# A kernel of 2068 ordered operations: 52 of them at other places, one copy of work given to another engine

## The chip, the cores and the metric

One core of a Trainium2 chip runs the whole kernel. Its engines are TensorE (PE, matmuls; its weight loads are listed as PEld), VectorE (DVE), ScalarE (ACT), GpSimd (POOL) and SyncE (SP), which issues the DMAs. The metric is the device time of one execution in microseconds; the time of before is the median of three runs.

## The reference

x has 2048 rows of 512. It is normalised row by row; the normalised rows go through a linear attention with 32 heads of 16 and through a feed-forward block of width 1792, and the output is x plus the product of the two.

```python
xn = _layernorm(x, axis=-1)
# attention: qkv = xn @ wqkv, per head:
pq = jnp.einsum("bhsd,hdf->bhsf", q, w_phi)
phi_q = jnp.concatenate([_softmax(pq, axis=-1), _softmax(-pq, axis=-1)], axis=-1)   # phi_k from k likewise
kv = jnp.einsum("bhsf,bhsd->bhfd", phi_k, v)
z  = jnp.einsum("bhsf->bhf", phi_k)
o  = einsum(phi_q, kv) / (einsum(phi_q, z) + 1e-6);  s = o @ wo
# feed-forward: h = xn @ w1 + b1, act = h * tanh(softplus(h))  (Mish), then act @ w2
g = _silu(_B_ref(xn, w1, b1, w2))
return x + s * g
```

Everything is float32.

## The kernel before, in words

**Tiles.** The 2048 rows are 16 tiles of 128 rows, x0 to x15. For each tile the program loads x, forms mean and variance (mv), 1/sqrt (rs, a power on GpSimd), normalises x in place, transposes it on TensorE in four pieces into a PSUM bank (pt), and copies that to SBUF as a high part (ScalarE) and a remainder (VectorE), together xT. The high and low parts of both factors make one float32 product out of three matmuls of a 128x512 result; a product over half the depth is six matmuls.

**Fewer products.** k and v, and likewise the two matmuls of the feed-forward block, are formed from sums of tiles and sums of weights, so that seven products do the work of eight. The sums of tiles t and t+4 are ts, split into th and tl; those of the weights are ws, split into wss by ScalarE (high) and GpSimd (low), and w1s, split into w1sh and w1sl. The running sums in PSUM are kx, ky and kz for k and v, fx, fy and fz for the first matmul of the feed-forward block, x, y and z for the second. A bank is copied out between two products (for fx: ha, hb, hc and hd, in that order), and the product that follows adds to it, so it waits for the copy.

**Attention.** For each tile of v there is a tile with one more column block of ones, which gives the sum z. That block is written by a copy of its own, of 16 columns, before the copy of v itself:

```python
def v_tile(t):
    v = alloc("s2", [P, H + 1, DH], f"v{t}")
    vp[t] = v
    copy(v[:, H], ones[:, 0:DH])
```

q of each tile goes out to DRAM (qs, qd) and comes back in another layout (qp). Later ez and tz form the denominators, ph the transposed features, pn the numerators, oh and ol their split, pw the product with wo, and so its copy, which goes out to DRAM.

**Start and end.** The first instructions on TensorE are matmuls of a tile of ones (wake), whose result nobody reads. The weights of q and k are multiplied by the feature map first (the folds wkf and wqf, from phit). At the end each output tile takes silu of its sum, times s, plus x.

**Order.** The program is not issued as it is written. Each call of an engine is recorded as one operation (or some calls as one: a product of six matmuls, four transposes), 2068 in all, numbered as recorded. A list, SCHED, then gives the order of issue. Where an operation was recorded for two engines (a copy for ScalarE or VectorE, a subtraction for VectorE or GpSimd, a normalisation for VectorE or ScalarE), a letter behind the number says which takes it: V, A or G. Each engine runs its own operations in the order of the list; an engine waits at an operation until what it reads is written and what it overwrites is read. A second list, PLACE, gives each of the 945 tiles its buffer within its pool (slot, s2, st, sm, rq, tq, and ps for the eight PSUM banks):

```python
for s in SCHED.split():
    i = int(s.rstrip("VGA"))
    op = self.ops[i]
    e = s.lstrip("0123456789") or next(iter(op))
    for m, a, k in op[e]:
...
        getattr(g, m)(*a, **k)
```

All operations are issued from one line, 192 of the kernel before, so the profile tells them apart by the names of their tiles and not by lines.

Of the kernel before, what the change touches and what calls it, by code (L numbers as in the profile page):

```python
# [49 lines left out]
0 1 2 3 4 5 6 7 8 25 26 27 11 12 9 10 15 13 64 36 28 29 30 31V 67A 65 16 37 39A 44 14 17 94 72 18 45 46 47 32 68 69 33  # L50
40 41 38 48 49 66 50A 34 73 74 43A 19 75 96 51 95 42 148 99 22 76 128 192 283 20 71A 118 172 55A 77 149 78V 79 21 70
193 100 52 80 23 97 129 56 130 53 57V 83 84 121 214 194 131 150 268V 85V 173 81 469 470 196 101 132 197 174 59 98 215
216 133 134V 24 58G 152 122 378 242 161G 189G 119 243 195 244 217 102 198 123G 162 104 164 135 136 139A 86 471V 87 379
381 89 137 176 140 177 246 88 245 284 285 247 142G 178 141V 103A 218 105 153 199 175 165 238 239 240A 287 114 286 143
# [21 lines left out]
604G 697 814 843 844 709 710 711 749 1100 665 692 785 784 786 799 798 742 698A 722 723G 699 763 741A 686 590 684 889
815 756 1054 1053 853 801 800 757A 855A 743 941 750 943 942 944 945 700 733 734 736 685 851V 852 817A 854A 735 752 744
766 767A 759 751 819 818 881 701 901 883 728 997 880 885 820V 845 823 753 754 821 737 888 822 891 788 1137G 865G 760A
846A 764A 769 758 848 946 947 1138 1139 738 1140 739 755 849 1141 1102 1142 866 775 768 1143 867 770A 824A 776A 761
1144 765 772 777 1145 827 887 847 996 1104 825 874 877 875A 830 1103 868 869 773 886 1105 828A 870 904 878 906 910 920  # L80
1106 903 1107 948G 856G 905 1108 831 771 790 882 826 774 893 890 1196 829 988 921A 857 858 907 908 909 949 871 986 911A
957 896 922 987A 1011 1012A 832 876 884 973 850 789 1197 778 879 950 951 1160 872 1109 787 1043 923 912 894 1025G 859
860 952 1052 861 862 953 1013 863 1022 864 762 995 1034 1023 895A 897 954 913 1024 1055 934 959 1019 1026 958A 1027
1028 1014 1112 935A 960 961A 1185G 974G 976G 1044G 1046G 975G 955 1029 1030 1111 924 898 956 962 1186 1056 1020A 936
1015 970 915 1036G 1058 1161 1187 873 1047V 1035V 1031 1016A 1032 914 1154 833 1048 916A 792 1017 1063 964 967 1039 971
1188 965V 791 1066 998 1147 1163 972 977G 1194 1195 1021 982 978 1067 1045G 1050 968A 983A 1040G 1049G 1076 966 1037V
794 1038V 1057 1059 1060 793 1033 1146 1110 1668 984 979V 1064V 1189 1190 1191 917 918 989 992 1051G 795 980 990A 981G
925G 1068 985 1018 963 1095 1006 1008 1650 991 1413 969 919 1638 1157 1061 993 1113 1192 1114 1041 1042G 796 1007A
1077A 1093 1069 1009 1062 1078 1094A 926 797 1116 927 1096 1115 1090 1091A 1124 1120 1155 1117 1070A 1072 1092 1081G
1082 1083 1084 928 1118 1085 1073A 1171 1567 929 1153 1097 1162 1412 1079 1086 1087 1088 1065 1121A 1125A 1127 1122  # L90
1158 1415 1010 1119 1211 1193 1199 930 931 932 1149 1198 1201 1164 1172A 1200 1134 1131 1071 1126 1156 1173 1148 1074
1132A 1128A 1129 1202 1639G 1260G 1651G 1165 999 1166 1167 1168 1568G 1569G 1669G 1269G 1135 1205 1208 1223 1224A 1174
1089 1203 1228 1214 1229A 1215A 1133 1414 1080 1175 1001 1209 1231 1206A 1232A 1204 1235 1216 1130 933 1416 1261 1000
1151 994 1159 1331 1136 1225 1002 1262 1263 1217 1236A 1244 1003 1177 1245A 1178A 1264 1004 1265 1417 1226 1418 1419
1152 1248 1599 1332 1075 1207 1123 1420 1238 1218 1266 1267 1005 1212 1333 1150 1227 1513 1239A 1169 1182 1179 1284
# [827 lines left out]
```

## Time and profile before

| | us |
|---|---|
| runs | 491.93, 492.81, 681.34 |
| median of the runs | 492.81 |
| profiled execution | 491.45 |
| its span | 489.71 |
| TensorE busy | 477.8 (98%) |
| VectorE busy | 448.3 (92%) |
| ScalarE busy | 292.5 (60%) |
| GpSimd busy | 267.2 (55%) |

The span runs from the first to the last instruction of the trace; the profiled execution's own time has 1.74 us more around it. The mean granted TensorE clock was 0.996 of full speed. In rows of the profile, an instruction is named by what it writes and what it reads, with the buffer numbers left out. TensorE's instructions are pipelined, so their modelled durations (0.39 us for a 128x512 matmul) overlap, and the distance between two starts is what counts. A row of the timeline gives start, duration, engine, line, operation, tiles, sizes, and the number of instructions that it groups; in square brackets stands the idle time before it and what ended it.

### The profile page before, as it was taken

To read this page: it belongs to the slowest core of one execution; us is meant where nothing else is said; L and a number is where in the kernel's file an instruction comes from. 1 tells how busy PE (TensorE), PEld (TensorE's weight loads), DVE (VectorE), ACT (ScalarE), POOL (GpSimd) and SP (SyncE) were. 2 spreads that over 40 slices of the span, in tenths; PEclk is the share of its full clock that TensorE was granted. 3 is DMA by queue.
4 is the path that set the end of the run, shared out by engine and by line. 5 is a ranking of instruction groups with operands and counts; after the bars stand their busy time and mean duration, and the time that the engine had idled before them with its cause. 6 is when DMAs were issued, how large, how long until landed. Compare 5 with 4: busy or idle time off the path is not lost.

```text
span 489.7 us, 9113 instructions
## 1 busy us (share of the span) xinstructions
PE 477.8 (98%) x3332; PEld 386.9 (79%) x3332; DVE 448.3 (92%) x716; ACT 292.5 (60%) x465; POOL 267.2 (55%) x185
## 2 busy tenths in 40 slices
PE   9999899999999999999999999999899999999995
PEld 9888678888787887888888867868678888888883
DVE  5989999999999999999999989999998977799965
ACT  5998675544262351325434558694795879889531
POOL 2678942323427333164825399968867647541540
PEclk9999999999999999999999999999999999999998
DMA  8524447595979777996999999972247747933276
GB/s 297 200 90 149 193 173 242 183 346 199 331 233 308 264 259 251 301 319 198 349 324 314 322 301 346 338 229 87 104 178 251 229 145 230 299 111 87 86 220 231
DMA packets 71133, 114.01 MB, mean 233 GB/s; under 512 B 6193, under 2 KB 39601, under 8 KB 71089
## 3 DMA queue, kind: packets, MB, share of 16 engines
q1 hardware_dynamic: 70944, 113.18, 68.8%
q8 instruction: 26, 0.43, 0.3%
q10 hardware_dynamic: 144, 0.26, 0.2%
q14 instruction: 19, 0.15, 0.1%
HBM read 71.47 MB, written 41.94 MB: 232 GB/s over the span
## 4 chain that ended last, share of the span: by engine, by line
PE 73%; DVE 10%; issue 3%; DMA 1%; ACT 1%; POOL 0%; DVEq 0%; SPq 0%; ACTq 0%
PE fx L192 16%; PE x L192 14%; PE y L192 8%; PE fy L192 7%; PE kx L192 6%; PE fz L192 4%; PE pw L192 4%; PE q L192 4%; PE ky L192 3%; PE z L192 2%; PE kvp L192 2%; PE kz L192 2%; DVE tz L192 1%; PE pn L192 1%; DMA so<-so 1%
## 5 line engine op out<-in xcount | busy, mean ns | idle before, releaser
L192 PE MATMUL q<-wqh,xT 128*128 128x512 f32 x128 | 42.2, 392 | 0.0
L192 ACT ACTIVATE r<-r,b1t 128x512 f32<-128x512 f32 x56 | 37.7, 713 | 0.1
L192 PEld LDWEIGHTS q<-wqh,xT 128*128 128x128 f32 x128 | 24.0, 188 | 5.2
L192 POOL TENSOR_TENSOR w1sl<-w1s,w1sh 128x1024 fp32r<-128x1024 f32 x7 | 16.8, 2406 | 20.1 <-ACT w1sh L192 16.4
L192 POOL TENSOR_TENSOR rs<-rs,mhalf 128x1 f32<-128x1 f32 x16 | 10.0, 641 | 29.4 <-DVE rs L192 25.1
L192 POOL TENSOR_TENSOR tl<-ts,th 128x1024 fp32r<-128x1024 f32 x8 | 19.4, 2431 | 10.4 <-ACT th L192 5.1
L192 PE MATMUL q<-wql,xT 128*128 128x512 f32 x64 | 25.0, 390 | 0.0
L192 DVE TENSOR_REDUCE tz<-ez 128x64 f32<-128x1024 f32 x16 | 19.3, 1208 | 0.3
L192 ACT ACTIVATE ha<-fx 128x512 f32<-128x512 f32 x14 | 8.2, 594 | 17.6 <-PE fx L192 14.0
L192 ACT ACTIVATE hd<-fx 128x512 f32<-128x512 f32 x13 | 7.7, 595 | 17.7 <-PE fx L192 14.4
L192 ACT ACTIVATE hc<-fx 128x512 f32<-128x512 f32 x13 | 7.6, 594 | 17.7 <-PE fx L192 17.7
L192 POOL TENSOR_TENSOR w1al<-w1a,w1ah 128x768 fp32r<-128x768 f32 x6 | 11.1, 1849 | 12.3 <-DMA scr<-xT 6.5
L192 PE MATMUL kx<-wss,th 128*128 128x512 f32 x56 | 17.6, 394 | 0.0
L192 ACT ACT_TABLE_LOAD x13 | 16.7, 1283 | 1.5 <-PEq L915 1.2
L192 ACT ACTIVATE hb<-fx 128x512 f32<-128x512 f32 x13 | 7.7, 595 | 13.8 <-PE fx L192 12.0
L192 ACT ACTIVATE kp<-kx 128x512 f32<-128x512 f32 x12 | 7.2, 596 | 14.7 <-PE kx L192 10.8
L192 POOL TENSOR_TENSOR mt<-r,r 128x512 f32<-128x512 f32 x7 | 9.5, 1364 | 11.6 <-ACT oh L192 4.4
L192 PE MATMUL pw<-oh,wo0l 128*128 128x512 f32 x32 | 12.6, 392 | 2.2 <-DVE h L192 2.2
L192 POOL TENSOR_TENSOR t<-r,mt 128x512 f32<-128x512 f32 x8 | 12.6, 1573 | 3.2 <-DVE mt L192 1.9
L192 PEld LDWEIGHTS q<-wql,xT 128*128 128x128 f32 x64 | 12.0, 188 | 2.5
L192 POOL TENSOR_TENSOR w2t<-w2t 128x512 f32<-128x512 f32 (+1 forms) x10 | 12.8, 1281 | 0.1
L192 PE MATMUL pw<-oh,wo0h 128*128 128x512 f32 x32 | 12.5, 389 | 0.0
(977 smaller groups left out, 1865.0 us busy)
## 6 DMA issues: line engine op xcount, KB each, us to landing
r<-hd SPq DMA_DIRECT2D x28, 512.0 KB, 5.5
qd<-qs SPq DMA_DIRECT2D x16, 256.0 KB, 4.0
scr<-xT SPq DMA_DIRECT2D x8, 512.0 KB, 6.3
scrT<-th SPq DMA_DIRECT2D x8, 512.0 KB, 4.3
scrT<-tl SPq DMA_DIRECT2D x8, 512.0 KB, 5.9
qp<-qd SPq DMA_DIRECT2D x64, 64.0 KB, 5.2
so<-so SPq DMA_DIRECT2D x16, 256.0 KB, 5.3
sr<-so SPq DMA_DIRECT2D x16, 256.0 KB, 3.6
```

Source lines behind the costliest of these rows:

```text
L192: getattr(g, m)(*a, **k)
```

## The change

The two lists have other numbers; the code and the operations are the same. 52 of the 2068 operations stand at other places, relative to those around them on their engine. One, number 200, the normalisation of tile x12, has the letter A in place of V: ScalarE does it, by an activation with a scale and a bias, in place of VectorE. In PLACE 110 of 945 tiles have another buffer after names are matched; where tiles trade numbers throughout, nothing changes but the number, and 72 tiles follow another tile in their buffer than before. A line of each list:

```diff
-120G 185 186 380 321 802 166V 288 289 290 151 219 200V 154 248 220 90 269 382 115 201 179 180V 187V 181 125 91 322 202
+120G 185 186 380 321 802 166V 288 289 290 151 219 154 248 220 90 200A 269 382 115 291V 292 201 179 180V 187V 181 125 91
...
-0 1 2 7 4 7 3 5 4 6 11 13 6 1 0 0 0 1 7 2 3 3 2 8 2 5 6 3 1 4 15 5 0 14 17 18 26 0 1 9 1 4 8 6 2 7 16 8 5 6 0 1 27 5 10
+0 1 2 7 4 7 3 5 4 6 11 13 6 2 0 0 0 1 7 2 3 3 2 8 2 5 6 3 1 4 14 5 0 13 16 18 26 0 1 9 1 4 8 6 2 7 17 8 6 5 0 2 27 5 10
```

The moves, by engine: on TensorE one wake matmul from the front to between two folds; the transposes of x7 from between two products of v to ahead of those of x12 and x8; those of x1 behind half a product and of x6 ahead of one; the product of ky7 with tl11 and wss0 ahead of one of kx6 and the second half of q11; a product of fx5 behind one of fx4; pw3 ahead of pw2. On VectorE x12's normalisation goes and x7's takes its place; some small steps of the softmaxes trade places. On ScalarE x12's normalisation comes in, a few copies trade places (xT4, x6, x3, hc5, two halves of w2x), and md0 and md1 move. On GpSimd the subtraction r1_0 comes forward from the stretch around 380 us to the one around 349, and some small steps trade places. On SyncE the load of x12 comes ahead of x5's and that of x7 behind the second load of wv.

VectorE, some 30 us into the program, where the tiles x7, x8 and x12 are normalised (mv and rs are their statistics, k0e and k0m belong to the softmax of k's first tile, qs5 is q of tile 5). Before:

```order
L192 TENSOR_SCALAR x12_245<-x12_245,mv12_246,rs12_249 128x512
L192 TENSOR_SCALAR nb8_240<-mv8_235,rs8_238 128x1
L192 TENSOR_SCALAR x8_234<-x8_234,mv8_235,rs8_238 128x512
L192 COPY qs5_242<-q5_243 128x512
L192 TENSOR_REDUCE k0m_186<-k0e_187 128x64
L192 TENSOR_SCALAR x7_294<-x7_294,mv7_295,rs7_298 128x512
```

Now:

```order
L191 TENSOR_SCALAR x7_294<-x7_294,mv7_295,rs7_298 128x512
L191 TENSOR_SCALAR nb8_240<-mv8_235,rs8_238 128x1
L191 TENSOR_SCALAR x8_234<-x8_234,mv8_235,rs8_238 128x512
L191 COPY qs5_242<-q5_243 128x512
L191 TENSOR_REDUCE k0m_186<-k0e_187 128x64
```

x12's normalisation is gone, and x7's has moved up by five rows to stand where it was.

TensorE at the same place, between the last product of q4 and the products of v0 and v4 (pt is the bank that the transposes write). Before, from the transposes of x8, with those of x12 in the row ahead:

```order
L192 MATMUL pt8_241<-ident_83,x8_234 128x128 x4
L192 MATMUL v0_208<-wv0h_202,xT0_153 128x512
L192 MATMUL v0_208<-wv0l_203,xT0_153 128x512
L192 MATMUL v0_208<-wv0h_202,xT0_153 128x512 x2
L192 MATMUL v0_208<-wv0l_203,xT0_153 128x512
L192 MATMUL v0_208<-wv0h_202,xT0_153 128x512
L192 MATMUL v0_208<-wv1h_205,xT0_153 128x512
L192 MATMUL v0_208<-wv1l_206,xT0_153 128x512
L192 MATMUL v0_208<-wv1h_205,xT0_153 128x512 x2
L192 MATMUL v0_208<-wv1l_206,xT0_153 128x512
L192 MATMUL v0_208<-wv1h_205,xT0_153 128x512
L192 MATMUL pt7_301<-ident_83,x7_294 128x128 x4
```

Now:

```order
L191 MATMUL pt7_301<-ident_83,x7_294 128x128 x4
L191 MATMUL pt12_252<-ident_83,x12_245 128x128 x4
L191 MATMUL pt8_241<-ident_83,x8_234 128x128 x4
L191 MATMUL v0_208<-wv0h_202,xT0_153 128x512
L191 MATMUL v0_208<-wv0l_203,xT0_153 128x512
L191 MATMUL v0_208<-wv0h_202,xT0_153 128x512 x2
```

The four transposes of x7 stand ahead of those of x12 and x8; they came after the products of v0.

TensorE some 140 us into the program, where the running sums kx6, ky6, kx7 and ky7 take their products and q11 is formed in two halves. Before:

```order
L192 MATMUL kx6_387<-wv1l_206,th10_402 128x512
L192 MATMUL kx6_387<-wv1h_205,th10_402 128x512
L192 MATMUL kx6_387<-wv1h_205,tl10_403 128x512
L192 MATMUL kx6_387<-wv1l_206,th10_402 128x512
L192 MATMUL kx6_387<-wv1h_205,th10_402 128x512
L192 MATMUL ky6_406<-wss2_288,xT14_397 128x512 x6
L192 MATMUL q11_410<-wqh1_145,xT11_356 128x512
L192 MATMUL q11_410<-wql1_146,xT11_356 128x512
L192 MATMUL q11_410<-wqh1_145,xT11_356 128x512 x2
L192 MATMUL q11_410<-wql1_146,xT11_356 128x512
L192 MATMUL q11_410<-wqh1_145,xT11_356 128x512
L192 MATMUL ky7_455<-wss0_229,tl11_422 128x512
```

Now:

```order
L191 MATMUL kx7_375<-wss2_288,tl11_422 128x512
L191 MATMUL kx7_375<-wss2_288,th11_421 128x512 x2
L191 MATMUL ky7_455<-wss0_229,tl11_422 128x512
L191 MATMUL ky7_455<-wss0_229,th11_421 128x512 x2
L191 MATMUL ky7_455<-wss0_229,tl11_422 128x512
L191 MATMUL ky7_455<-wss0_229,th11_421 128x512 x2
L191 MATMUL kx6_387<-wv1h_205,tl10_403 128x512
L191 MATMUL kx6_387<-wv1l_206,th10_402 128x512
L191 MATMUL kx6_387<-wv1h_205,th10_402 128x512
L191 MATMUL kx6_387<-wv1h_205,tl10_403 128x512
L191 MATMUL kx6_387<-wv1l_206,th10_402 128x512
L191 MATMUL kx6_387<-wv1h_205,th10_402 128x512
```

The product of ky7 stands directly behind that of kx7, which reads the same tl11 and th11, and ahead of the last product of kx6 and the second half of q11. ky6's product, in the row after, is where it was.

More of the change, by code (lines that the diff above doesn't have):

```diff
@@ L49 @@
 SCHED = """
[L50 to L54, printed above, removed]
-120G 185 186 380 321 802 166V 288 289 290 151 219 200V 154 248 220 90 269 382 115 201 179 180V 187V 181 125 91 322 202
-291V 323 203 155 126 292 228 190 249 92 93 116A 264 265 205A 206 107 191G 505 167 188 144 182 156V 208G 207V 250A 506
-221 222A 293 127A 472 183 209 106 474 145G 235 270G 325 266A 109 294 108 296V 223 297 157 236A 251 229 255A 158 224 110
+0 1 2 3 4 5 6 7 8 9 25 26 27 11 12 15 13 64 36 28 29 30 31V 67A 65 16 37 39A 44 14 17 94 72 18 45 46 47 32 68 10 69 33
+40 38 48 49 66 50A 34 73 74 43A 41 19 75 96 51 42 95 148 22 76 99 192 128 20 71A 118 172 55A 77 149 21 78V 70 193 52
+100 23 97 129 56 194 53 130 57V 83 79 80 84 121 283 214 131 150 268V 196 197 85V 173 81 469 470 101 132 174 59 98 215
+216 133 134V 24 58G 152 122 378 242 198 161G 189G 119 243 195 244 217 102 123G 162 104 164 135 136 139A 86 471V 87 89
+379 381 137 176 140 177 246 88 245 284 285 247 142G 178 141V 103A 218 105 153 199 175 165 238 239 240A 287 114 286 143
+120G 185 186 380 321 802 166V 288 289 290 151 219 154 248 220 90 200A 269 382 115 291V 292 201 179 180V 187V 181 125 91
+322 202 323 203 155 126 228 190 249 92 93 116A 264 265 205A 206 156V 107 191G 505 167 188 144 208G 207V 250A 182 506
+293 127A 472 183 221 222A 209 106 474 145G 251 235 270G 325 266A 109 294 108 296V 223 297 157 236A 229 255A 158 224 110
 317 159 326 298G 299G 256 508 473 111 300 225 112 60 319A 252 267 541 54 241 340 226 160 138 655 656 334G 305 335 507
@@ L76 @@
[L76 to L95, printed above, removed]
@@ L131 @@
-1993 2009 2004 2010 2005 2065 1888 2039 2057 2053 2061 2054 2066 2062 2058 2063 2011 2059 2055 2067 2035 2040 2036 2041
-2042 2037 2038
+677A 670 672 694A 500 499 716V 673 537 693 674 234 561 690 747 501 565A 675 462 566 661 627 526 837 902 679 683 745 601
+502 503 461 809 695A 629A 617 538 539A 681 504 464 463 618 839 841 600G 619 620 713V 628A 780 782 779 781 783 587 662
+663 718G 717G 719G 622 838 840 621 465 564A 645 646G 712 588 842 623 714A 589A 664V 813 466 696 624 702 467 625 626 892
+540 680 811 602G 940 687 691 562 703 724 812A 725A 705 721G 704 468 726 706 707 727 708 598G 603 810G 740 816 604G 697
@@ new lines @@
+814 843 844 709 710 711 749 1100 665 1099 692 785 784 786 799 798 742 698A 722 723G 699 763 741A 686 590 684 889 815
+756 1054 1053 750 853 801 800 757A 855A 743 941 943 942 944 945 700 733 734 736 685 851V 852 817A 854A 735 752 744 766
+767A 759 751 819 818 881 701 901 883 728 997 880 885 820V 845 823 753 754 821 737 888 822 891 788 1137G 865G 760A 846A
+764A 769 758 848 946 947 1138 1139 738 1140 739 755 849 1141 1102 1142 866 775 768 1143 867 770A 824A 776A 761 1144 765
+772 777 1145 827 887 847 996 1104 825 874 877 875A 830 1103 868 869 773 886 1105 828A 870 904 878 906 910 920 1106 903
@@ new lines @@
+1107 948G 856G 905 1108 831 771 973 790 882 826 774 893 890 1196 829 988 921A 857 858 907 908 909 949 871 986 911A 957
+896 922 987A 1011 1012A 832 876 884 850 789 1197 778 879 950 951 1160 872 1109 787 1043 923 912 894 1025G 859 860 952
+1052 861 862 953 1013 863 1022 864 762 995 1034 1023 895A 897 954 913 1024 1055 934 959 1019 1026 958A 1027 1028 1014
+1112 935A 960 961A 1185G 974G 976G 1044G 1046G 975G 955 1029 1030 1111 924 898 956 962 1186 1056 1020A 936 1015 970 915
+1036G 1058 1161 1187 1047V 1035V 873 1031 1016A 1032 914 1154 833 1048 916A 792 1017 1063 964 967 1039 971 1188 965V
@@ new lines @@
+1057 791 1066 998 1147 1163 972 977G 1194 1195 1021 982 978 1067 1045G 1050 968A 983A 1040G 1049G 1076 966 1037V 794
+1038V 1059 1060 793 1033 1146 1110 1668 984 979V 1064V 1189 1190 1191 917 918 989 992 1051G 795 980 990A 981G 925G 1068
+985 1018 963 1095 1006 1008 1650 991 1413 969 919 1638 1157 1061 993 1113 1192 1114 1041 1042G 796 1007A 1077A 1093
+1069 1009 1062 1078 1094A 926 797 1116 927 1096 1115 1090 1091A 1124 1120 1155 1117 1070A 1072 1092 1081G 1082 1083
+1084 928 1118 1085 1073A 1171 1567 929 1153 1097 1162 1412 1079 1086 1087 1088 1065 1121A 1125A 1127 1122 1158 1415
@@ new lines @@
+1010 1119 1211 1193 1199 930 931 932 1149 1198 1201 1164 1172A 1200 1134 1131 1071 1126 1156 1173 1148 1165 1074 1132A
+1128A 1129 1202 1639G 1260G 1651G 999 1166 1167 1168 1568G 1569G 1669G 1269G 1135 1205 1208 1223 1224A 1174 1089 1203
+1228 1214 1229A 1215A 1133 1414 1080 1175 1001 1209 1231 1206A 1232A 1204 1235 1216 1130 933 1416 1261 1000 1151 994
+1159 1331 1136 1225 1002 1262 1263 1217 1236A 1003 1177 1178A 1264 1004 1265 1417 1226 1418 1419 1152 1248 1599 1332
+1075 1207 1123 1420 1238 1218 1266 1267 1005 1212 1333 1150 1227 1513 1239A 1169 1182 1244 1245A 1179 1284 1180 1302G
@@ new lines @@
+1570 1183A 1421 1422 1285A 1213G 1670V 1219 1251 1324 1170 1303 1304 1671 1600G 1601G 1672V 1305 1306 1220A 1256 1258
+1259 1252 1403G 1230 1184 1233 1330 1240 1521 1278 1249 1254 1253 1255 1335 1640G 1257 1286 1659 1299 1241 1237 1279A
+1234 1442 1210 1652G 1571G 1653 1641 1445G 1242 1290 1334 1221 1336 1325 1246 1654G 1250G 1660G 1280 1181 1341 1291
+1293 1602 1300 1307 1337 1308 1338 1294 1292 1295 1281 1287 1309 1282 1270 1314 1384 1374 1661G 1514G 1301G 1662 1663G
+1515G 1516 1517G 1326G 1537 1642G 1436 1297 1437A 1454 1247 1363 1438 1553 1222 1342 1464 1603V 1296 1446 1310 1271
@@ new lines @@
+1272 1447 1298 1268 1339 1448 1360 1361V 1273 1364 1423 1357 1315 1283 1532 1381 1376 1343 1316 1317 1382A 1481 1523
+1344 1348G 1318G 1345G 1327 1328A 1522 1443 1424 1404 1288 1321 1538 1439 1311 1349 1405 1449 1340 1350 1406 1407 1351
+1408 1444G 1409 1396 1243 1289 1450 1352 1274 1275 1451 1452 1353 1276 1354 1429 1366 1329 1176 1539 1358 1312A 1456
+1482 1375 1455 1385 1377 1524G 1525G 1277 1359V 1410 1322V 1386V 1425V 1426 1533G 1527G 1534G 1790 1355 1356 1427V 1430
+1440A 1535 1398 1431 1397 1555 1399 1493 1483V 1378G 1536V 1463 1462 1319 1320 1540G 1400V 1541V 1347 1346 1379 1484
@@ new lines @@
+1494 1432 1411 1433G 1789 1714 1461 1763 1457 1441 1380 1487 1548 1383 1365 1489 1485 1543G 1458G 1453 1488 1491 1495
+1496 1466 1492 1402 1435 1401 1434 1460 1465 1468 1467 1486 1490 1469 1367 1368 1369 1370 1497G 1542G 1472G 1371 1313
+1428 1323 1607 1470 1459 1498 1502V 1499 1372 1473 1503 1373 1564 1565V 1528 1387G 1604 1388 1471 1474 1475 1476 1605V
+1544 1554 1500A 1791 1572 1744 1389 1390 1792 1391 1793 1529G 1526G 1545G 1745A 1703 1556G 1574 1573 1623 1762 1606
+1588 1583 1609 1608 1704A 1530 1531 1547 1624 1477 1392 1393 1394 1478 1549G 1479 1557G 1550G 1551 1559G 1575G 1576G
@@ new lines @@
+1560 1480 1501 1395 1579 1561V 1552V 1504 1546 1580V 1562 1581 1509 1589 1511 1507 1505 1584G 1512 1578V 1510 1508
+1558V 1506 1563 1582 1764 1625 1698 1765 1610G 1680 1618 1729 1705 1611G 1613G 1626V 1614 1766 1591V 1627V 1629G 1628V
+1585V 1615V 1586 1590 1587V 1566 1362 1768 1794 1746 1735 1592G 1594V 1619G 1620G 1647 1648A 1595 1596V 1518 1726 1677
+1727A 1621 1622V 1681G 1715 1630 1612V 1631V 1577V 1643 1655 1664 1769 1673 1597 1598 1617 1633 1616 1728 1775 1720
+1689 1767 1637A 1721 1635A 1665V 1850 1699V 1644V 1656V 1717 1770 1632 1682G 1683 1716G 1636V 1722V 1706 1694 1674G
@@ new lines @@
+1645 1657 1666 1690G 1691V 1649 1782 1833 1634A 1646 1684V 1593V 1692 1777 1685 1835 1776 1686V 1658 1667 1675 1676
+1730 1738 1687 1688 1784 1783 1771 1519A 1695V 1700V 1701 1872 1845 1809 1795 1718G 1693G 1707G 1696 1702G 1697 1772V
+1678V 1773 1774 1709 1739V 1736 1778 1785 1708 1779G 1781 1851 1873 1852 1834 1796 1802 1786V 1731V 1780 1787 1788 1712
+1811 1797 1723 1798 1710 1713 1853V 1855V 1854V 1520 1737G 1724G 1911 1912 1750 1799V 1822 1801 1800 1810 1874 1804
+1719 1803 1805 1679 1846 1711 1806G 1732 1812 1913 1889 1756 1844 1983 1994 1741 1861 1917 1807 1808 1725 1813V 1836V
@@ new lines @@
+1753 1824 1823 1825 1733G 1838G 1837G 1754V 1847 1875V 1914 1839V 1759 1900 1965 1815 1814 1734 1826V 1828 1827 1891
+1742 1877V 1856G 1760V 1862 1751 1747 1971 1743V 1864V 1748V 1876V 1915 1752V 1829V 1857 1970 1964 1863 1866G 1902 1757
+1758G 1840 1740 1865V 1848 1841V 1858V 1749 1755 1761 1817 1901 2015 1831A 1890 1842 1859 1843 1860 1832 1879 1868
+1880V 1869V 1871 1870 1881 1882 1984 1972 1985 1892G 1916 1893G 1896 1897V 1899 1830 1973 1974 1903V 2016V 1904V 1918
+2012 1919 1920G 1921V 1905V 1895V 1898 1966 1849 1976 1982 1977 1975 1907 1908V 1924 1936 1932 1818 1910 1925V 1927
@@ new lines @@
+1937V 1894V 1986 1922V 1933V 1909 1952 1931A 1929A 1926 1956 1940 1978 1957V 1941V 1967 2013V 1944 1930A 1934 1938 1942
+1928A 1945G 1885 1948 2024 1935 2025V 1979 1949V 1968 1980 1923V 1819 1816 1987 1884 1886 1989 1969 1981 2001 1953G
+1867G 2018 2019G 1939 1943 1947 1946 1950 1954 1958 1962 1878G 2030 1996 1951 1955 2043 1959 1906V 2027 2028V 2021
+2022G 1820 1960 2031G 1961 2002 2050 1995 2033 1988 1883 1990 2007 2000 2051 2006 1963 1997 2003 1991 1992 1998 2044
+2045 2046 2047 2048 2008 2014 2017 2049 2052 2064 2060 2056 2020 2023 2026 2029 2032 1887 1999 1821 2034 1993 2009 2004
@@ L133 @@
+2010 2005 2065 1888 2039 2057 2053 2061 2054 2066 2062 2058 2055 2063 2011 2059 2067 2035 2040 2036 2041 2042 2037 2038
 """
 PLACE = """
[20 rows of a table removed]
[20 rows of a table added]
 """
```

43 lines of the change are left out of this document (2 added, 41 removed), and 38 rows, old and new, of the table PLACE.

## The prediction

> **What bounds it now.** I read the page first, then what each engine waited for, then the stretches, then single rows of the timeline. Lines 1 and 2 of the page:
>
> ```profile
> span 489.7 us, 9113 instructions
> PE 477.8 (98%) x3332; PEld 386.9 (79%) x3332; DVE 448.3 (92%) x716; ACT 292.5 (60%) x465; POOL 267.2 (55%) x185
> ```
>
> TensorE is the bound, with VectorE close behind. No operation is added or removed, so a new order can win only TensorE's idle time: 489.7 - 477.8 = 11.9 us, start and tail included. The view of waits lists what of it has a cause:
>
> ```profile
> PE pw L192 <- DVE h L192: 2.2, 1, 2.2
> PE kz L192 <- DVE v L192: 1.4, 1, 1.4
> PE wake L192 <- DVE mhalf L274: 1.1, 1, 1.1
> PE pn L192 <- DVE ph L192: 0.5, 1, 0.5
> PE kx L192 <- issue: 0.5, 1, 0.5
> ```
>
> These are 5.7 us in all. A measurement of this kernel can tell about 2% from no change, which is 9.8 us here: faster by 2% would need every one of these waits and most of the tail, so it is as good as excluded. What can be forecast is a change of one or two microseconds. Two stretches where TensorE is not full, and one where it is (us, then busy and count of PE, PEld, DVE, ACT, POOL, then granted clock, DMA share, GB/s):
>
> ```profile
> 45.00:60.00 15.00, 13.57 (x59) 10.77 (x59) 14.33 (x28) 11.79 (x22) 14.35 (x12) 1.00 0.63 227
> 320.00:347.00 27.00, 24.30 (x158) 18.22 (x157) 26.76 (x30) 19.26 (x25) 20.25 (x10) 1.00 0.46 146
> 347.00:395.00 48.00, 48.00 (x264) 37.94 (x264) 43.47 (x55) 34.13 (x49) 34.84 (x25) 1.00 0.59 195
> ```
>
> Where PE fills its stretch, work added to another engine costs nothing unless it makes PE wait. So I ask of each moved piece only whether a PE instruction then starts later than its predecessor allows. The dense rate comes from a row of the chain, 24 matmuls in 5.44 us, 0.227 us each, 1.36 us for a product of six:
>
> ```profile
> 102.14 5.44 PE q L192 x24
> ```
>
> **The wake matmul.** Eleven pairs of records come first; one moves between two of the folds.
>
> ```profile
> 1.12 4.47 PE L192 MATMUL wake<-ones 128*128 128x128 f32 x22 [1.12 <-DVE mhalf L274]
> 4.61 0.68 DVE L192 TENSOR_TENSOR phit<-phic,bmask 128x512 f32<-128x512 f32 x1
> 5.43 0.85 PE L192 MATMUL wkf<-phit,wkT 128*128 128x128 f32 x6
> ```
>
> The first fold needs phit, which ends at 5.29, so one wake fewer gains at most 5.43 - 5.29 = 0.14 at the front. Put in later it costs two records: by the mean of the row's 22, 4.47/22 = 0.20 each, 0.4 at most; by the 0.85/6 = 0.14 of the folds 0.28, which I take, as the clock is the folds' there. Net +0.15 to +0.3, until the wait at 51 us swallows it.
>
> **The stretch from 30 to 53 us.** PE waits 1.4 us at 52.86 for a VectorE copy. Rows of PE, VectorE and GpSimd there:
>
> ```profile
> 51.04 0.39 PE L192 MATMUL kx<-wkh,xT 128*128 128x512 f32 x1
> 52.86 0.50 PE L192 MATMUL kz<-wkh,xT 128*128 128x512 f32 x1 [1.43 <-DVE v L192]
> 49.88 2.33 DVE L192 COPY v<-ones 128x16 f32<-128x16 f32 x1
> 52.13 0.68 DVE L192 COPY v<-v 128x512 f32<-128x512 f32 x1
> 49.09 0.74 POOL L192 TENSOR_TENSOR ts<-xr,ts 128x256 f32<-128x256 f32 x1
> 49.80 4.74 POOL L192 TENSOR_TENSOR wss<-ws,wss 128x1024 fp32r<-128x1024 f32 x2
> L192 DVE COPY v<-ones 128x16 f32<-128x16 f32 x4 | 4.5, 1133 | 0.0
> ```
>
> A copy of 16 columns took 2.33 us. It started 0.08 us after GpSimd's wss and ended at 52.21, when the first of the two wss (4.74/2 = 2.37) ended. Its like at 147.48 (below) took 1.54; the other two of the four share 4.5 - 2.33 - 1.54 = 0.6, 0.3 each. So the copy was held by GpSimd's instruction, and started 0.1 us sooner it would have been done in 0.3. [...]
>
> What the change does ahead of it: x12's normalisation goes from VectorE to ScalarE, x7's takes its place, and x7's transposes now stand ahead of x12's and x8's on PE.
>
> ```profile
> 33.47 1.04 PE L192 MATMUL pt<-ident,x 128*128 128x128 f32 x8
> 34.10 0.60 ACT L192 ACTIVATE xT<-pt 128x512 fp32r<-128x512 f32 x1 [0.71 <-PE pt L192]
> 34.81 0.68 DVE L192 TENSOR_TENSOR xT<-pt,xT 128x512 fp32r<-128x512 f32 x1
> L192 DVE TENSOR_SCALAR x<-x,mv,rs 128x512 f32<-128x512 f32 x8 | 4.9, 610 | 0.0
> L192 ACT ACTIVATE x<-x,nb,rs 128x512 f32<-128x512 f32 x8 | 6.4, 809 | 0.0
> ```
>
> ScalarE takes 0.81 us for x12, of which 0.71 fall into its idle time at 34.10. VectorE loses 0.61, but has to wait: four transposes ahead (about 1.04/2 = 0.5; I take 0.43, as the tail of the last is pipelined) plus the wake's 0.2 put pt12, ScalarE's xT12 and VectorE's xT12 at 34.81 + 0.6 = 35.4. The sums for GpSimd hang on VectorE:
>
> ```profile
> 45.29 0.75 POOL L192 TENSOR_TENSOR ts<-xr,ts 128x256 f32<-128x256 f32 x1 [1.53 <-DVE ts L192]
> ```
>
> From 45.29 on GpSimd has no gap until 54.5 (14.35 us busy in 45 to 60), so a later start passes through to wss: I take +0.47 (0.6 less 0.13 that VectorE makes up), so that ts is at 49.56 to 50.30 and wss at 50.27. VectorE's copy at 49.88 then meets the short ts, waits at most until 50.30, and is done by 50.35 to 50.6; v's copy follows (0.6), by 51.0 to 51.5, held back at most by PE's own kx at 51.04 + 0.23. kz starts between 51.5 and 52.3 where it started at 52.86: a gain of 0.6 to 1.4, and 1.0 is taken. If VectorE comes 0.4 us later than I work out, wss holds it again, now until 52.65: +0.45.
>
> **The product moved at 143 us.** ky7's product from tl11 and wss0 goes ahead of three others, so q11's second half ends 1.36 us later, and with it a row of ScalarE and GpSimd work:
>
> ```profile
> 143.46 0.60 ACT L192 ACTIVATE qs<-q 128x512 f32<-128x512 f32 x1 [2.19 <-PE q L192]
> 145.47 1.04 ACT L192 ACTIVATE w1sh<-w1s 128x1024 fp32r<-128x1024 f32 x1
> 146.59 2.40 POOL L192 TENSOR_TENSOR w1sl<-w1s,w1sh 128x1024 fp32r<-128x1024 f32 x1 [9.35 <-ACT w1sh L192]
> 147.48 1.54 DVE L192 COPY v<-ones 128x16 f32<-128x16 f32 x1
> 153.00 0.39 PE L192 MATMUL q<-wqh,xT 128*128 128x512 f32 x1
> 153.51 0.50 PE L192 MATMUL fz<-fb1h,w1al 128*128 128x512 f32 x1
> ```
>
> Waiting behind qs on ScalarE are k11's exponential and w1sh; w1sl on GpSimd then starts up to 1.36 later, of which I let ScalarE make up 0.2 to 0.4 between these: 147.6 to 147.8, an estimate. VectorE's copy of ones starts at 147.48. So it now comes first by 0.1 to 0.3 us and takes 0.3 in place of 1.54, and the 153.51 - 153.00 - 0.23 = 0.28 us that fz waits goes; or it comes second, waits for w1sl's end at 150.0 where it ended at 149.02, and fz starts up to 1.0 later. I take the first: -0.3, with +1.0 as the other end.
>
> **fx5's products at 270 to 280 us.** fx5's second product now comes after fx4's, and ScalarE's copy hc5 stands behind hd6; fx5's third product must wait for hc5.
>
> ```profile
> 279.01 0.57 ACT L192 ACTIVATE hd<-fx 128x512 f32<-128x512 f32 x1
> 279.96 0.39 PE L192 MATMUL fx<-ft3h,w1al 128*128 128x512 f32 x1
> ```
>
> hc5 ends at 279.01 + 0.57 + 0.57 = 280.15, 0.2 us after the product could start: +0.2, at most 0.6 if hd6 is late by as much.
>
> **297 to 347 us.** Here VectorE sets the end (26.76 of 27.00 us busy) and PE waits twice. pw3 and pw2 change places, and ScalarE's half of w2x stands ahead of oh and so.
>
> ```profile
> 300.13 0.60 ACT L192 ACTIVATE so<-pw 128x512 f32<-128x512 f32 x1 [0.64 <-PE pw L192]
> 302.65 0.39 PE L192 MATMUL pw<-oh,wo0l 128*128 128x512 f32 x1
> 320.45 3.49 DVE L192 TENSOR_TENSOR w2x<-w2r,w2x 128x512 fp32r<-128x512 f32 x2
> 320.95 2.44 POOL L192 TENSOR_TENSOR ma2l<-r,ma2h 128x1024 fp32r<-128x1024 f32 x1 [1.56 <-ACT ma2h L192]
> 329.18 2.89 DVE L192 TENSOR_TENSOR mt<-r,mt 128x512 f32<-128x512 f32 x1
> ```
>
> so goes from 300.13 to about 302.3, so that the pw product at 302.65 may wait 0.2 for its bank; the wait before 346.71 covers that, 2.2 us long. VectorE itself loses two of its times to the same kind of meeting (2.89 for the second w2x and for mt, against 0.6 for the first: 3.49 - 2.89). GpSimd's stream comes about 0.35 later, which may keep both, add one or spare one: 0 taken, ±2.3 (2.89 - 0.6) as the bounds.
>
> **The rest at nothing.** GpSimd's subtract r1_0 comes earlier in the stretch from 347 to 395, and other work there moves by its length; this lies where PE has no gap (48.00 of 48.00). A few loads on SyncE's queue change places; x7, moved furthest, goes behind x8's and both of wv; were it late, PE would wait at its transposes, which come at 33.47 now. The last pieces of the output keep their last matmul and what follows it.
>
> **The sum.** Wake 0 after the wait; 30 to 53: -1.0; 143: -0.3; 280: +0.2; 297 to 347: 0. Together -1.1. The profiled execution took 491.45 (span 489.71 and 1.74 around it), which gives 490.3. The runs of before are 491.93 and 492.81, with a third far off (681.34), so the median 492.81 is the upper of two. The profiled time and these two lie about 492.1: I forecast 492.1 - 1.1 = 491.0.
>
> **Rivals.**
> - *Nothing reaches PE.* Behind kz's wait stands another (v's ones on ScalarE, or the kx products themselves), and what is won at 51 us is given back in the waits of pn and pw, which VectorE sets. For it: VectorE is 14.33 of 15 us busy there. Against: the view of waits has no other PE wait before pn and pw but 0.5 of issue, so what is won at 51 us is kept for a while. Time 491.5 to 492.5; chance 0.27.
> - *Slower: the copies of ones come second both times.* The point is whether VectorE's copy starts before GpSimd's wss (margin 0.4) and before w1sl (margin 0.1 to 0.3). Both lost cost +0.45 + 1.0 + 0.2 = +1.65, and one more meeting in 320 to 347 +2.3: 493.7, up to 496. For it: the margins are smaller than the shifts I worked out. Chance 0.22, of which 0.03 for five or more new meetings of 2.3 us each, the number it takes to pass 2%.
> - *Faster by more.* One meeting spared in 320 to 347 as well takes off the 2.2 us of the wait of pw: 488.9. Chance 0.08.
>
> My own forecast (490 to 491.5) has 0.43. Range: from 488.9, the spared meeting, to 494.4, which is 492.1 and one meeting of 2.3 added; it leaves out the far part of the slower case. Faster by over 2% 0.01, slower by over 2% 0.03, within 2% 0.96.
>
> **What would show it.** Right: the copy of ones near 50 us takes 0.3 to 0.8 us, kz's wait falls below 0.9, w1sl starts after the copy near 147.5, and PE's waits come to about 4.5 us. Wrong: the copy takes 2 us again; pw's wait before 346 differs by more than 1 us; or PE waits at a place that is dense now, above all at the transposes of x7, which stand in front of eight others.

## The result, and the profile after

The changed kernel takes 486.11 us (median of four runs, 485.23 to 486.61). The kernel before took 492.81 beside it (the median of 491.93, 492.81 and 493.93; a fourth run, at 681.34, is left out of the comparison). The ratio is 0.986 with a 95% interval of 0.983 to 0.989: 1.4% faster, 5.3 to 8.5 us. The forecast was 491.0, in a range of 488.9 to 494.4: the sign was right, the size (1.1 us) was a sixth of the 6.7 us that came, and the time lies below the range.

The changed kernel's span and busy times from its page, then the view of what TensorE waited for, whole:

```profile
span 484.9 us, 9103 instructions
PE 477.2 (98%) x3332; PEld 388.1 (80%) x3332; DVE 442.2 (91%) x715; ACT 293.0 (60%) x466; POOL 264.0 (54%) x185
PE wake L191 <- DVE mhalf L273: 1.1, 1, 1.1
PE kx L191 <- issue: 0.4, 1, 0.4
```

TensorE is busy for the same time (477.2 against 477.8), and the span is 4.8 us shorter. The waits of kz (1.4), pw (2.2) and pn (0.5) are gone, 4.1 of the 4.8. VectorE, with the same work but one normalisation (0.5 us), is busy 6.1 us less. The stretches that were shown of before:

```profile
45.00:60.00 15.00, 15.00 (x71) 12.37 (x70) 14.71 (x33) 12.85 (x23) 13.29 (x12) 1.00 0.68 245
320.00:347.00 27.00, 27.00 (x174) 20.98 (x173) 26.06 (x40) 20.64 (x27) 23.80 (x12) 1.00 0.42 136
347.00:395.00 48.00, 48.00 (x265) 38.14 (x264) 41.11 (x47) 37.21 (x53) 29.60 (x23) 1.00 0.62 195
```

TensorE fills all three. In 320 to 347 it ran 174 matmuls where it ran 158. Around 50 us, VectorE, GpSimd and TensorE:

```profile
51.03 0.46 DVE L191 COPY v<-ones 128x16 f32<-128x16 f32 x1
51.41 0.68 DVE L191 COPY v<-v 128x512 f32<-128x512 f32 x1
50.72 0.74 POOL L191 TENSOR_TENSOR ts<-xr,ts 128x256 f32<-128x256 f32 x1
51.42 4.78 POOL L191 TENSOR_TENSOR wss<-ws,wss 128x1024 fp32r<-128x1024 f32 x2
52.22 0.39 PE L191 MATMUL kx<-wkh,xT 128*128 128x512 f32 x1
52.45 0.39 PE L191 MATMUL kz<-wkh,xT 128*128 128x512 f32 x1
```

The copy of ones now meets the short ts and takes 0.46 us where it took 2.33, and kz follows kx without a gap. Around 320 us, ScalarE, VectorE and GpSimd of the changed kernel:

```profile
318.16 0.62 ACT L191 ACTIVATE w2x<-w2r 128x512 fp32r<-128x512 f32 x1
318.81 1.29 DVE L191 TENSOR_TENSOR w2x<-w2r,w2x 128x512 fp32r<-128x512 f32 x2
319.81 2.57 POOL L191 TENSOR_TENSOR ma2l<-r,ma2h 128x1024 fp32r<-128x1024 f32 x1 [1.01 <-ACT ma2h L191]
325.92 0.69 DVE L191 TENSOR_TENSOR mt<-r,mt 128x512 f32<-128x512 f32 x1
326.38 2.49 POOL L191 TENSOR_TENSOR ma4l<-r,ma4h 128x1024 fp32r<-128x1024 f32 x1 [2.74 <-ACT ma4h L191]
```

The two w2x take 1.29 us where they took 3.49, and mt 0.69 where it took 2.89. The second w2x starts at 318.81 + 0.6 = 319.4, 0.4 us ahead of ma2l; before it started at 321.05, 0.1 us behind ma2l's 320.95. With mt it is the same: it starts 0.46 us ahead of ma4l now, and before stood 0.92 us behind it, as this row of the kernel before shows beside mt at 329.18:

```profile
328.26 3.26 POOL L192 TENSOR_TENSOR ma4l<-r,ma4h 128x1024 fp32r<-128x1024 f32 x1 [3.16 <-DMA so<-so]
```

ma4l takes 3.26 us there and 2.49 now: it had itself started 0.22 us behind VectorE's ma3l (328.04 to 329.26), so GpSimd seems to be held by VectorE as well.

That is where 4.4 us of VectorE's time went, and with it the waits of pn and pw. In what follows, a meeting is such a case: a VectorE instruction that starts just behind a long one of GpSimd and is held by it.

### The profile page after: what moved, and what is told of

Its sections match the earlier page's. It is cut to its first block, busy times and chain, and to the rows that moved or that the text cites. A ratio compares the mean times of both kernels' runs of the same rounds, so it can differ in the third digit from the quotient of the medians.

```text
span 484.9 us, 9103 instructions
## 1 busy us (share of the span) xinstructions
PE 477.2 (98%) x3332; PEld 388.1 (80%) x3332; DVE 442.2 (91%) x715; ACT 293.0 (60%) x466; POOL 264.0 (54%) x185
## 4 chain that ended last, share of the span: by engine, by line
PE 98%; DVE 0%; ACT 0%; issue 0%; DVEq 0%
PE fx L191 16%; PE x L191 16%; PE q L191 9%; PE pw L191 9%; PE kx L191 8%; PE fy L191 8%; PE y L191 8%; PE ky L191 4%; PE fz L191 4%; PE z L191 4%; PE kvp L191 2%; PE kz L191 2%; PE pn L191 2%; PE pt L191 2%; PE k L191 1%; PE v L191 1%
## 5 line engine op out<-in xcount | busy, mean ns | idle before, releaser
L191 PEld LDWEIGHTS kx<-wss,th 128*128 128x128 f32 x56 | 10.5, 188 | 3.2 <-issue 0.8
```

## The experiments

The list can be cut at each place where the old and the new list have issued the same operations. So kernels can be made that follow the new list (and its buffers) in one stretch and the old list elsewhere. **Theory:** the gain is the end of three meetings (49.9, 321 and 329 us), each ended by the moves near it. **Rival:** the lead that is won in the first 50 us separates the two engines later as well. All times are medians of three rounds; the ratio is to the kernel before, run beside it. e5, e6 and e11 to e14 keep the buffers of before and change its order list alone.

| kernel | us | ratio and interval | waits of TensorE on kz, pn, pw |
|---|---|---|---|
| before, beside e1 to e4 | 492.57 | | 1.4, 0.5, 2.2 |
| e1, new order to 45 us | 490.64 | 0.996 (0.994 to 0.998) | 0, 0.5, 2.2 |
| e2, new order 290 to 310 us | 489.03 | 0.993 (0.990 to 0.995) | 1.4, 0, 0.3 |
| e3, new without the first | 487.70 | 0.989 (0.985 to 0.992) | 1.4, 0, 0 |
| e4, new without the second | 489.49 | 0.994 (0.992 to 0.996) | 0, 0.5, 2.2 |
| e5, so4 two places later | 487.87 | 0.991 (0.988 to 0.993) | 1.4, 0, 0 |
| e6, two copies to ScalarE | 490.28 | 0.995 (0.993 to 0.997) | 0, 0.5, 2.2 |
| e7, e1 and e2 together | 486.76 | 0.988 (0.986 to 0.991) | 0, 0, 0.2 |
| e8, new order 130 to 167 us | 492.69 | 1.001 (0.999 to 1.003) | 1.4, 0.5, 2.2 |
| e9, pw3 ahead of pw2 alone | 493.45 | 1.000 (0.998 to 1.003) | 1.4, 0.4, 2.3 |
| e10, moves of w2x alone | 489.17 | 0.993 (0.990 to 0.995) | 1.4, 0, 0.6 |
| e11, e5 and e6 together | 486.27 | 0.987 (0.984 to 0.990) | 0, 0, 0 |
| e12, pw's wait made longer | 494.77 | 1.002 (1.000 to 1.004) | 1.4, 0.5, 3.0 |
| e13, h's addition sooner | 493.07 | 1.001 (0.999 to 1.003) | 1.4, 0.5, 0.2 and 1.8 |
| e14, e11 with a wait made | 489.25 | 0.993 (0.991 to 0.996) | 0, 0, 2.5 |

**e1 and e3: the first 45 us.** The part of the list up to there, alone and taken out; of its lines the one with x12:

```diff
-120G 185 186 380 321 802 166V 288 289 290 151 219 200V 154 248 220 90 269 382 115 201 179 180V 187V 181 125 91 322 202
+120G 185 186 380 321 802 166V 288 289 290 151 219 154 248 220 90 200A 269 382 115 291V 292 201 179 180V 187V 181 125 91
```

> The kernel before, with the new order (and the new buffers) for the first 45 us alone: wake, the moves of x7, x12 and pt7, x12's normalisation on ScalarE. Theory (three meetings of VectorE and GpSimd, at 49.9, 321 and 329 us, each removed by the moves near it): the wait of kz goes, span about 1.5 us less than before, the waits of pn and pw stay (0.5 and 2.2). Rival (the lead won early is what separates the two engines later): the waits of pn and pw go too, span 4 to 5 us less.

> The new kernel, with the old order for the first 45 us. Theory: only the wait of kz comes back, span 1.5 us more than the new kernel's. Rival: kz, pn and pw all wait, span 4 to 5 us more.

e1 ended kz's wait and nothing else: kz starts at 51.85 where it started at 52.86. In e3 only kz's wait came back, and it took 1.6 us more than the new kernel. The rival falls: with the early lead alone, w2x near 321 still took 2.89 us and mt 2.89.

**e2 and e4: 290 to 310 us.** The part of the list from there, alone and taken out; its core (1515 is w2s0, 1516 and 1517 are the two halves of w2x0_2, 1360 is pw3, 1361 so3's copy, 1381 pw2):

```diff
-1662 1663G 1326G 1515G 1537 1642G 1436 1297
...
-1448 1273 1364 1423 1357 1315 1283 1532 1516 1381
...
-1344 1517G 1348G 1318G 1345G 1360 1361V 1327
+1662 1663G 1515G 1516 1517G 1326G 1537 1642G 1436 1297
...
+1448 1360 1361V 1273 1364 1423 1357 1315 1283 1532 1381
...
+1344 1348G 1318G 1345G 1327
```

> The kernel before, with the new order for the operations of 290 to 310 us alone (w2x, w2s, pw3 and pw2, ph0). Theory: the wait of kz stays at 1.4, those of pn and pw go, span about 3 us less. Rival (lead won earlier): pn and pw wait as before, span as before within 0.5 us.

> The new kernel, with the old order for the operations of 290 to 310 us. Theory: kz does not wait, the waits of pn and pw come back, span 3 us more than the new kernel's. Rival: none of the three waits comes back, span as the new kernel's.

As the theory said, both times: alone it saves 3.5 us, without it the new kernel is 3.4 us slower. The view of waits of e4, its rows without the wake:

```profile
PE pw L191 <- DVE h L191: 2.2, 1, 2.2
PE pn L191 <- DVE ph L191: 0.5, 1, 0.5
```

**e9 and e10: which of these moves.** pw3's, with so3's copy and the banks that it needs, alone (e9, the edit here); then those of w2x alone, with the old order of pw2 and pw3 (e10: the moves of 1515, 1516 and 1517 above, and of 1325, a half of w2x1_0):

```diff
-1448 1273 1364
+1448 1360 1361V 1273 1364
...
-1345G 1360 1361V 1327
+1345G 1327
```

> The kernel before with pw3 ahead of pw2 on TensorE, and so3's copy with it, alone (with the PSUM banks and buffers that this needs). If the swap is what matters in 290 to 310 us: w2x near 321 takes 0.7, pn and pw do not wait, 3 to 4 us less. If not: 2.9 at 321 and at 329, and pw waits 2.2 as before.

> The kernel before with the moves of w2x1_0, w2s0 and w2x0_2 on ScalarE and GpSimd in 290 to 310 us alone, pw2 ahead of pw3 as before. If these matter: 0.7 at 321, no wait of pn and pw, 3 to 4 us less. If not: as before.

It is the w2x moves. VectorE and GpSimd of e9, then of e10:

```profile
320.06 3.50 DVE L192 TENSOR_TENSOR w2x<-w2r,w2x 128x512 fp32r<-128x512 f32 x2
320.60 2.41 POOL L192 TENSOR_TENSOR ma2l<-r,ma2h 128x1024 fp32r<-128x1024 f32 x1 [1.59 <-ACT ma2h L192]
```

```profile
322.24 1.29 DVE L192 TENSOR_TENSOR w2x<-w2r,w2x 128x512 fp32r<-128x512 f32 x2 [0.79 <-ACT w2x L192]
323.24 2.58 POOL L192 TENSOR_TENSOR ma2l<-r,ma2h 128x1024 fp32r<-128x1024 f32 x1 [1.66 <-ACT ma2h L192]
```

In e10 VectorE waits for ScalarE's half of w2x, which ma2h follows on ScalarE and ma2l follows that. So it starts at once when ScalarE is done and is ahead of ma2l by 0.4 us. In e9, as before, VectorE comes late enough that its second w2x (320.06 + 0.6 = 320.66) falls 0.06 us behind ma2l. Two things bring that about. VectorE's w2x near 300 us took 1.33 us before, 0.82 in the new kernel and 1.19 in e10. And in e10 ScalarE's stream comes later: its half of w2x, now ahead of oh and so, waits 2.93 us for GpSimd's w2s at 302.51, so's copy comes late behind it, and TensorE waits 0.6 in all for so's copies. So the wait that was priced as a cost of 0.2 helps to keep the two apart; how much each of the two things does was not measured alone.

**e5 and e6: the meetings without the change.** One operation moved, and two letters changed, in the list of before:

```diff
-1358 1312A 1456 1482 1375 1455 1385 1377 1524G 1525G 1277 1359V 1410 1322V 1386V 1425V 1426 1533G 1527G 1534G 1790 1355
+1358 1312A 1456 1482 1375 1455 1385 1377 1524G 1525G 1277 1359V 1410 1386V 1425V 1322V 1426 1533G 1527G 1534G 1790 1355
```

> The kernel before with one operation moved: VectorE's copy so4 (0.68 us) behind the two w2x instead of ahead of them. By the meetings (w2x at 321.05 lost to GpSimd's ma2l by 0.1 us; ma2l follows ScalarE and does not come sooner), w2x starts 0.5 us sooner and takes 0.7 in place of 2.9; then mt comes ahead of ma4l as well and takes 0.7 in place of 2.9; the waits of pn and pw go, 2.9 us less. Rival (the meetings are not the cause, VectorE's sum of work is): VectorE's work is the same, the waits stay, span as before within 0.5 us.

```diff
-509 227A 124V 230V 475
+509 227A 124A 230V 475
...
-619 620 713V 628A
+619 620 713A 628A
```

> The kernel before with two copies of ones (those at 49.88 and 147.48) given from VectorE to ScalarE, in place. By the meetings: kz waits no longer, nor fz at 153.5 (0.28); span 1.5 to 1.9 us less, the waits of pn and pw stay. Rival (a second wait stands behind kz's): kz waits 0.5 us or more on something else, span less than 1 us shorter.

e5 saves 4.3 us in a single move. VectorE and GpSimd of e5:

```profile
319.99 1.29 DVE L192 TENSOR_TENSOR w2x<-w2r,w2x 128x512 fp32r<-128x512 f32 x2
327.12 0.69 DVE L192 TENSOR_TENSOR mt<-r,mt 128x512 f32<-128x512 f32 x1
320.99 2.57 POOL L192 TENSOR_TENSOR ma2l<-r,ma2h 128x1024 fp32r<-128x1024 f32 x1 [1.58 <-ACT ma2h L192]
327.56 2.51 POOL L192 TENSOR_TENSOR ma4l<-r,ma4h 128x1024 fp32r<-128x1024 f32 x1 [2.74 <-ACT ma4h L192]
```

Nothing was moved near mt, and yet its meeting is gone too: the first meeting, ended, brings VectorE 2.1 us ahead (mt at 327.12 in place of 329.18), and so in front of ma4l. The two are one chain. In e6 kz does not wait, and no second wait stood behind it.

**e7, e8 and e11: what is in the sum.** e7 is e1 and e2 in one; e11 is e5 and e6 in one, by the edits shown; e8 has the new list for 130 to 167 us alone (661 is ky7's product, 538 the second half of q11, 589 the copy qs13, 1099 a load of qp7):

```diff
-462 566 627 526 837 902 679 683 745 601 502 503 461 809 695A 629A 617 538 539A 661 681
...
-1099 703 589A 724 812A
+462 566 661 627 526 837 902 679 683 745 601 502 503 461 809 695A 629A 617 538 539A 681
...
+623 714A 589A 664V
...
+665 1099 692 785
```

> The kernel before with both pieces of the change that were run alone: the first 45 us and 290 to 310 us. If these are the change, its time is that of the new kernel within 0.7 us, that is 486.1 to 487.5; if the moves between (ky7, fx5) matter for more, 488 or more.

> The kernel before with the new order for 130 to 167 us alone (ky7's product). If the copy of ones at 147.48 now comes ahead of w1sl: it takes 0.2 to 0.3 us in place of 1.54, fz waits 0.28 less, span 0.3 to 0.6 less. If it comes second: fz waits 1.0 us more.

> The kernel before with so4 two places later on VectorE and the two copies of ones on ScalarE, nothing else of the change. By the meetings neither kz nor pn nor pw waits; the gains of the two alone add up: -4.4 and -1.9, about 486.0, as the new kernel or a little less.

e7 is within 0.65 us of the new kernel by the medians, and the intervals of the two overlap, so no more than that can be told of the rest of the change. In e8 the copy of ones came ahead of w1sl, VectorE and GpSimd:

```profile
147.46 0.17 DVE L191 COPY v<-ones 128x16 f32<-128x16 f32 x1
147.63 2.41 POOL L191 TENSOR_TENSOR w1sl<-w1s,w1sh 128x1024 fp32r<-128x1024 f32 x1 [10.44 <-ACT w1sh L191]
```

fz's wait of 0.28 us is gone, though the time, 492.69, shows no gain that can be told. e11, three numbers of the old list, takes 486.27 us: as much as the 52 moves.

**e12, e13 and e14: TensorE's clock.** The waits in the trace came to 4.1 us, but the time fell by 6.7. In the profile of e1, which still has pw's wait, matmuls behind it start 0.427 us apart in place of 0.227 for some 3 us, and the granted clock is 0.65 from 348 to 352 us. In those of e4 and e6, which have it too, the clock falls at the same place: to 0.57 from 344 to 348 us in e4, to 8 tenths in the slice from 343 to 355 us on e6's page. In the profile of before it does not, 1.00 from 344 to 352 us:

```profile
346.71 0.50 PE L192 MATMUL pw<-oh,wo0l 128*128 128x512 f32 x1 [2.23 <-DVE h L192]
347.04 0.39 PE L192 MATMUL pw<-ol,wo0h 128*128 128x512 f32 x1
```

The runs of kernels with this wait spread over 3 us: of the 21 of before beside e1, ten lie between 491.0 and 492.3 and eleven between 492.6 and 494.6. So I made the wait longer by two reciprocals ahead of h's addition (1503), then took it away by moving that addition ahead of two reductions, and then made one in e11, where there are no meetings:

```diff
-1499 1372 1473 1503 1373 1564 1565V 1528 1387G 1604 1388 1471 1474 1475
+1499 1372 1473 1373 1471 1503 1564 1565V 1528 1387G 1604 1388 1474 1475
```

> The kernel before with two reciprocals (0.55 us each) ahead of h's addition on VectorE, so that pw's wait is 3.3 us in place of 2.2. Theory (a wait of 2.2 us lets TensorE's clock fall to half for some 3 us in a part of the executions, which costs 1.5 more): with 3.3 us it falls in most or all, every run near 495, half clock in the trace behind the wait. Rival (the two groups of times of the kernel before have another cause): the runs spread as before, 1.1 us later, 492.5 and 495.

```diff
-1499 1372 1473 1503 1373 1564 1565V
+1499 1503 1372 1473 1373 1564 1565V
```

> The kernel before with h's addition on VectorE moved ahead of two reductions, directly behind the copy of h, so that pw does not wait for it; the meetings at 321 and 329 us (2.9 us each) stay. If the wait is what lets TensorE's clock fall: pw's wait of 2.2 goes, no execution has half clock behind it, mean clock 0.996 or more, the runs within 1.5 us of each other, near 489 (the faster runs of before, 491.0 to 492.3, less 2.2). If it is the meetings: the runs still lie in two groups some 2 us apart.

```diff
-1499 1372 1473 1503 1373 1564 1565V 1528 1387G 1604 1388 1471 1474 1475
+1499 1372 1473 1373 1564 1565V 1528 1387G 1388 1503 1604 1471 1474 1475
```

> e11 (neither meetings nor waits behind 45 us, its runs 486.1 to 487.3 at clocks of 0.996 to 0.998) with h's addition on VectorE put behind so11's copy and a reduction, so that pw waits for it some 2 to 2.4 us where it did not wait. If the wait lets TensorE's clock fall: a part of the runs at clocks of 0.995 and less, and some 2 us above the others: two groups near 488.5 and 490.5. If the meetings did: every run at 0.996 or more, within 1.5 us of 488.5.

TensorE in e12, then in e14:

```profile
344.68 0.39 PE L192 MATMUL pw<-oh,wo1h 128*128 128x512 f32 x1
348.08 0.80 PE L192 MATMUL pw<-oh,wo0l 128*128 128x512 f32 x1 [3.02 <-DVE h L192]
348.68 0.63 PE L192 MATMUL pw<-ol,wo0h 128*128 128x512 f32 x1
349.10 0.63 PE L192 MATMUL pw<-oh,wo0h 128*128 128x512 f32 x1
```

```profile
341.42 0.39 PE L192 MATMUL pw<-oh,wo1h 128*128 128x512 f32 x1
344.31 0.79 PE L192 MATMUL pw<-oh,wo0l 128*128 128x512 f32 x1 [2.50 <-DVE h L192]
344.90 0.63 PE L192 MATMUL pw<-ol,wo0h 128*128 128x512 f32 x1
345.33 0.63 PE L192 MATMUL pw<-oh,wo0h 128*128 128x512 f32 x1
345.75 0.63 PE L192 MATMUL pw<-oh,wo0l 128*128 128x512 f32 x1
```

In e12 the longer wait (3.0 us, 3.3 was meant) let the clock fall in seven of ten runs: three took 491.9 to 493.1 at a mean clock of 0.999, seven 494.1 to 496.5 at 0.990 to 0.995. "Most or all" held, "every run near 495" did not. In e14, without the meetings, four runs took 488.5 to 489.3 at 0.996 to 0.999 and three 489.8 to 490.5 at 0.995: so a wait alone does it. The two groups lie 1.3 us apart by their means, not the 2 that was expected. e13 missed its aim: the wait did not go but moved on to a later product of pw, as its view of waits shows, and its runs still lie in two groups (four at 491.6 to 491.9, six at 493.0 to 494.3), so it does not tell wait from meeting.

```profile
PE pw L192 <- DVE q15r L192: 1.8, 1, 1.8
PE pw L192 <- DVE h L192: 0.2, 1, 0.2
```

What it does tell is that not h's place on VectorE is late there but VectorE itself.

The mean clock of a run has to be read with care. It also counts the time behind TensorE's last matmul, where a fall costs nothing (the clock was 0.68 there in the kernel before, from 484 to 490 us). Of the 82 runs of before beside the experiments, those at 0.997 or more took 492.2 us at most and those at 0.995 or less 492.3 at least, but at 0.996 there are both, from 491.1 to 494.6: the profile of before has 0.996 without the fall behind pw's wait, that of e9 has 0.996 with it. The 22 runs of e2, e3, e5, e7 and e10, in which TensorE waits 1.4 us at the longest behind the start, all have clocks of 0.996 to 0.999; the three at 0.996 are not the slowest of their kernels, and on the pages of their five profiles the clock is at 9 tenths or more in each of the first 39 slices of 40, up to 472 us, where a fall as behind pw's wait in e6 or e9 shows as an 8.

## Why the prediction was wrong, point by point

- **The bound** (only TensorE's idle time can be won, and faster by 2% is as good as excluded): right in direction, but "5.7 us in all" was the sum of one execution, in which the clock had not fallen. A wait can cost its length and then some 1.5 us more: in e14's trace, behind a wait of 2.5 us, one matmul starts 0.59 and five 0.43 us after the last in place of 0.23, and the seventh still 0.31: 0.36 + 5 x 0.2 + 0.08 = 1.4. This time counts as busy (TensorE is busy 479.7 us in e1's profile, 477.8 in that of before), so a sum of idle time cannot hold it.
- **The wake matmul** (0.15 to 0.3 more until the wait at 51 us swallows it): no gain at the front, where at most 0.14 was allowed: the first fold started at 5.54 in place of 5.43. The loss was swallowed, as said.
- **30 to 53 us** (-1.0): right, and by its steps. The copy met the short ts and took 0.46 (at most 0.7 was said), where the one at 146.90 us in the new kernel took 0.17. It ended 0.03 us behind ts, in the new kernel (51.49 and 51.46) as in e1 (50.90 and 50.87), so ts did hold it. In e1 kz started 1.01 us sooner. GpSimd came later than worked out (ts 1.04 us in e1, 0.47 was said), VectorE too (0.56), so the order held. By time e1 saved 1.9 us, interval 1.1 to 3.1, which leaves the forecast 1.0 just outside.
- **143 us** (-0.3, with +1.0 as the other end): the step held to the tenth. w1sl was put at 147.6 to 147.8 and came at 147.63 in e8, behind the copy; fz's wait went. Its worth was too small to be seen in the time.
- **fx5 at 280 us** (+0.2): mis-sized, measured 0. hc ends in the new kernel at 278.29, and TensorE's product starts at 278.57 without a gap: ScalarE was 0.4 us further ahead there than before.
- **297 to 347 us** ("0 taken, ±2.3 as the bounds"): this is the step that failed. It measured -3.5 us in e2 and -3.4 between e4 and the new kernel. One of the prediction's own signs of being wrong is what came: pw's wait before 346 differed by more than 1 us. Three things were wrong in it. The margin stood in the rows that were quoted: the second w2x, at 320.45 + 0.6, came 0.1 us behind ma2l, at 320.95. A meeting with so small a margin goes either way at shifts of 0.3 us, but "one meeting spared" got a chance of 0.08. Then the two meetings were taken for separate, each worth 2.3, where ending the first ends the second (e5). And GpSimd's stream was said to come 0.35 later as if alone; what decides is VectorE's start against ScalarE's stream, which ma2l follows.
- **The rest at nothing**: right, as far as the 0.65 us between the medians of e7 and the new kernel can tell.
- **The base** (492.1, from the profiled time and two runs): medians of the kernel before, beside the experiments, were 492.2 to 493.6. The mean of three looked over the two groups of times that go with the clock (in e1 488.95 to 490.79 us at 0.996 or more, 491.50 to 492.38 at 0.995 or less), so the sum was set off from 0.1 to 1.5 us too low.
- **The rivals:** the one that came was "faster by more", priced at 488.9 (by its terms, 491.0 - 2.2, it is 488.8). It had the 2.2 us of pw and not the 0.5 of pn nor the clock behind the wait. "Nothing reaches PE" and "slower" had half the chance; e1 and e6 show that what is won at 51 us is kept, and that no second wait stands behind kz's.

## What to carry to other kernels

Where two engines hold each other up, list for every lengthened instruction by how much it started behind the one that held it: a margin of 0.1 us beside a cost of 2 us is worth a single move of one operation, and here two such edits did as much as 52 moves. Follow each one on along its engine, since an ended meeting shifts everything behind it and can end or make the next. A meeting is worth something only where the bounding engine then waits: two instructions of VectorE (me), 0.68 us each alone, take 5.33 us together beside two long ones of GpSimd in both kernels, at 457 us before and at 452 now, and TensorE is busy throughout from 440 to 460 us. And count a wait of the bounding engine at more than its length where the clock can fall behind it (1.4 us more in e14's trace); one profiled execution need not show that, as that of before did not.
